# Loading the last unit of the output projection in three pieces: a half, a quarter and a quarter

## The chip, the cores and the metric

The kernel runs on one core of one Trainium2 chip. The metric is the device time in microseconds (us) of one execution. All runs quoted here are "fast" (within 1.5% of the fastest run of the same kernel). Beside the time, a run has a *span*, the time from the first to the last instruction of the profile; clock times such as "385.95" are microseconds from the start of that span.

Engines by the profile's names: PE is TensorE, DVE is VectorE, ACT is ScalarE, POOL is GpSimd, SP is SyncE, which here only issues loads. "16 engines" always means the 16 DMA engines that move the data. Each of them adds one to a load's semaphore (a counter) when it has finished its part; a load has *landed* when the sixteenth increment is there.

## The reference

One decode step of grouped attention, added to a small gated mixer. Cut to what matters:

```python
x = A_x                                            # [1, 1, 1024]
g = sigmoid((x * gate_w).sum(-1))
q = x @ wq                                         # 32 heads of 128
scores = einsum(q, k_cache) * 128 ** -0.5          # 4 kv heads, 65536 keys each
o = softmax(scores) @ v_cache                      # 32 x 128 = 4096 numbers
a = o @ wo                                         # wo: [4096, 1024]: "the output projection"
b = mixer(x, w_in, w_sp, b_sp, w_out)
return g * a + (1 - g) * b
```

There is one query, so every byte of the caches and weights (162 MB) is read once and used a few times: the kernel is a stream of loads with arithmetic behind it. `wo` (8 MB) comes last, because it is multiplied with the attention's result.

## The kernel before

All large loads go through one list, `stream`. The SP engine issues them in order into a ring of five slots (`NS = 5`); an issue waits until the former contents of its slot have been used. `wo` is four units of 2 MB, 16 KB of each of the 128 partitions.

```python
    for i in range(4):
        load([("wo", i)], [(0, rows(A_wo, i, 8))])
    # ... (cut)
    def issue(upto):
        while issued[0] < min(upto, len(stream)):
            n = issued[0]
            # ... (cut)
            P("SP", f, w=[("slot", s)], dma="s%d" % s)   # f: dma_start into slot n % NS
            issued[0] += 1
    # ... (cut)
    def done(key):                                       # called when a unit has been used
        n = place[key][0]
        if key == stream[n][0][-1]:
            issue(n + NS + 1)
```

The end of the program multiplies the four units with the attention's result `ovec` and adds the mixer's row `brow`:

```python
    FB = KTB[0]
    for i in range(4):
        sl, key = use(("wo", i))
        def f(e, i=i, sl=sl):
            for c in range(8):
                for q in range(4):
                    ins = e.matmul(pf(FB)[32 * q:32 * q + 1, 0:QW], ovec[:, 8 * i + c:8 * i + c + 1],
                                   sl[:, DO * c + QW * q:DO * c + QW * (q + 1)],
                                   start=(i == 0 and c == 0), stop=(i == 3 and c == 7), tile_position=(0, 32 * q),
                                   skip_group_check=True)
            return ins
        P("PE", f, r=[("ovec", i), key], w=[B(FB)])      # waits for the whole unit
    P("DVE", lambda e: e.tensor_tensor(orow[0:97, :], pf(FB)[0:97, 0:QW], brow[0:97, :], ALU.add),
      r=["brow"], w=["orow", B(FB)])
    # ... (cut) SP stores orow to the output
```

The four matmuls of one `c` use four different column groups of the array. In the trace they start within 15 ns of each other: below they are called a *round*. A unit is 8 rounds.

Of the kernel before, what the change touches and what calls it, by code (L numbers as in the profile page):

```python
# [137 lines left out]
def bass_gated_mix__gqa_block_cached__mixer_gmlp__decode_kernel(  # L138
# [19 lines left out]
    DO = A_wo.shape[1]  # L158
# [13 lines left out]
    QW = DO // 4  # L172
# [54 lines left out]
    def slot(n):  # L227
        return ab("RING", SLOT, (n % NS) * SLOT)
# [15 lines left out]
    def B(i):  # L244
        return ("bank", i)
# [12 lines left out]
    def small(dst, src, key):  # L258
        def f(e):
            with nc.allow_non_contiguous_dma(reason="a few bytes"):  # L260
                return e.dma_start(dst, src)
        P("ACT", f, w=[key], dma=key)
# [11 lines left out]
    def load(keys, pieces):  # L274

        for i, key in enumerate(keys):
            place[key] = (len(stream), i)
        stream.append((keys, pieces))

    def rows(w, i, c):  # L280

        return w[128 * c * i:128 * c * (i + 1), :].rearrange("(p c) n -> p (c n)", c=c)
# [28 lines left out]
    for n in range(NU, total + NU + 1):  # L311
# [7 lines left out]
        else:  # L319
            v = None  # L320
        steps.append((k, v, ()))
    for i in range(4):
        load([("wo", i)], [(0, rows(A_wo, i, 8))])

    WIDTH = {"wq": 2 * WQ_N, "win": 2 * F, "wout": 7 * DO, "wo": 8 * DO, "k": UK, "v": UK}
    issued = [0]
# [2 lines left out]
# [3 lines that stand above are left out]
            assert n < NS or all(k in used for k in stream[n - NS][0])  # L332
            keys, pieces = stream[n]
            s = n % NS

            def f(e, n=n, pieces=pieces):
                for c0, src in pieces:
                    ins = e.dma_start(slot(n)[:, c0:c0 + src.shape[1]], src)
                return ins
            P("SP", f, w=[("slot", s)], dma="s%d" % s)  # L340
            issued[0] += 1

    def use(key):
        n, i = place[key]
        issue(n + 1)
        used.add(key)
        w = WIDTH[key[0]]
        return slot(n)[:, i * w:(i + 1) * w], ("slot", n % NS)

    def done(key):  # L350
# [4 lines that stand above are left out]
# [25 lines left out]
    for i in range(4):  # L380
        sl, key = use(("wq", i))

        def f(e, i=i, sl=sl):
            for k in range(2):
                for h in range(HQ):
                    ins = e.matmul(pf(OB)[:, h:h + 1], sl[:, WQ_N * k + 128 * h:WQ_N * k + 128 * (h + 1)],  # L386
                                   xT[:, 2 * i + k:2 * i + k + 1], start=(i == 0 and k == 0 and h == 0),
                                   stop=(i == 3 and k == 1), skip_group_check=True)
            return ins
        P("PE", f, r=["xT", key], w=[B(OB)])  # L390
        done(("wq", i))
# [220 lines left out]


    FB = KTB[0]
    for i in range(4):
        sl, key = use(("wo", i))

        def f(e, i=i, sl=sl):
            for c in range(8):
                for q in range(4):  # L620
                    ins = e.matmul(pf(FB)[32 * q:32 * q + 1, 0:QW], ovec[:, 8 * i + c:8 * i + c + 1],  # L621
                                   sl[:, DO * c + QW * q:DO * c + QW * (q + 1)],
                                   start=(i == 0 and c == 0), stop=(i == 3 and c == 7), tile_position=(0, 32 * q),
                                   skip_group_check=True)
            return ins
        P("PE", f, r=[("ovec", i), key], w=[B(FB)])
    P("DVE", lambda e: e.tensor_tensor(orow[0:97, :], pf(FB)[0:97, 0:QW], brow[0:97, :], ALU.add),
      r=["brow"], w=["orow", B(FB)])
    osrc = bass.AP(tensor=arena, offset=OFF["OROW"], ap=[[32 * NA, 4], [1, QW]])
# [31 lines left out]
```

## Time and profile before

| | before |
|---|---|
| time, median of the first 3 runs | 392.74 us (392.17 to 393.21) |
| span of the profiled run | 390.4 us |
| load queue's share of the 16 engines' span | 97.1% |
| PE busy | 274.1 us, 70% |
| last load's last byte reported | 385.81 |
| last 32 matmuls | 385.95 to 387.83 |
| final add starts | 387.88 |

From the page of the kernel before: the DMA busy share in 40 slices of the span (tenths, 9 is 90% or more), the packet count, and two of the DMA queues (packets, MB, share of the 16 engines' span). Queue 1 carries the loads; queue 8 carries instructions.

```profile
DMA  8999999999999999999999999999999999999992
...
DMA packets 6778, 162.54 MB, mean 416 GB/s; under 512 B 1492, under 2 KB 1496, under 8 KB 1496
...
q1 hardware_dynamic: 5912, 162.01, 97.1%
q8 instruction: 30, 0.49, 0.5%
```

The kernel is bound by its loads. The digits are 9 from the second slice to the second last, and queue 1 alone takes 97.1%. What can be saved without moving fewer bytes is looked for here at the end of the stream. The end, from the chain of waits (start us, us, what):

```profile
361.59 24.22 DMA arena<-in_A_wo_dram
385.81 0.14 issue
385.95 1.91 PE pb L621 x32
...
387.88 0.42 DVE arena L627
```

The PE waits for unit 3 until 385.81, then does 1.91 us of matmuls, then the add follows. The timeline of the same stretch (start us, us, engine, line, operation, output<-input, count, and in brackets the idle time before it and what ended it):

```profile
374.50 3.58 PE L621 MATMUL pb<-arena 128*1 128x256 bf16 x64
...
380.99 1.04 PE L621 MATMUL pb<-arena 128*1 128x256 bf16 x32 [2.92 <-DMA arena<-in_A_wo_dram]
...
385.95 1.88 PE L621 MATMUL pb<-arena 128*1 128x256 bf16 x32 [3.91 <-DMA arena<-in_A_wo_dram]
387.88 0.42 DVE L627 TENSOR_TENSOR arena<-pb,arena 97x256 bf16<-97x256 f32 x1 [12.56 <-PE pb L621]
```

Units 0 and 1 run together at 374.50 because their data was there before the PE was free. Units 2 and 3 each wait for their load. Unit 3's group takes 1.88 us where unit 2's identical group took 1.04 us. The windows show the granted clock and the DMA share:

```profile
core 0: us, PE busy (x) PEld busy (x) DVE busy (x) ACT busy (x) POOL busy (x), PEclk, DMA share, GB/s
375.00:380.00 5.00, 3.08 (x60) 1.60 (x52) 0.32 (x1) 0.00 (x0) 0.00 (x0) 0.63 1.01 433
380.00:385.00 5.00, 1.04 (x32) 0.67 (x32) 0.00 (x0) 0.00 (x0) 0.00 (x0) 0.72 0.51 220
385.00:391.00 6.00, 1.88 (x32) 0.96 (x32) 0.42 (x1) 0.00 (x0) 0.00 (x0) 0.50 0.00 0
```

The last three columns are the granted TensorE clock, the DMA share and GB/s. The clock is a mean over the stretch. The trace's clock records have it at 1.0 from 378.74 to 382.16, while unit 2's group ran, and at 0.5 afterwards, while unit 3's ran: hence 1.04 and 1.88 us for the same work. From 375 to 380 all engines work (a share of about 1.0). From 380 to 385 only half the capacity is used, although unit 3 is still arriving. The reason is in the trace's records of semaphore increments. For unit 3 the first increment came at 380.48 and the sixteenth at 385.81. The engines run 5.3 us apart, and the load counts as there when the slowest is done.

### The profile page before, as it was taken

What the parts mean: (1) busy time and instruction counts of PE and PEld (TensorE: products, weight loads), DVE (VectorE), ACT (ScalarE), POOL (GpSimd) and SP (SyncE); (2) the same over time, 40 slices, a digit from 0 to 9 for tenths busy, and PEclk for the clock granted to TensorE, in tenths of its full rate; (3) what the DMA queues carried; (4) which work ended last, traced back from release to release, by engine and by line L of the source; (5) the groups of instructions that cost most, each with busy time, mean ns of one, the idle gap of its engine ahead of it and who ended that gap; (6) DMA issues with size and microseconds to landing.
All of it is one profiled execution on the core that took longest, in us unless ns stands there. A gap on an engine that the chain in (4) does not pass through costs nothing.

```text
span 390.4 us, 8502 instructions
## 1 busy us (share of the span) xinstructions
PE 274.1 (70%) x3902; PEld 194.6 (50%) x3902; DVE 160.2 (41%) x347; ACT 124.4 (32%) x171; POOL 1.5 (0%) x8
## 2 busy tenths in 40 slices
PE   0000699996999899976787596957974959574552
PEld 0000678885776676745565474645743736221121
DVE  2000043435666666644664263536742636410020
ACT  1000033332556555551355151613551425231000
POOL 1000000000000000000000000000000000000000
PEclk9999998685999999996899598968995989856555
DMA  8999999999999999999999999999999999999992
GB/s 322 430 430 437 418 412 441 426 428 425 411 405 431 433 426 431 428 431 428 427 431 428 428 431 430 425 435 435 428 431 433 428 426 431 433 431 421 416 415 96
DMA packets 6778, 162.54 MB, mean 416 GB/s; under 512 B 1492, under 2 KB 1496, under 8 KB 1496
## 3 DMA queue, kind: packets, MB, share of 16 engines
q1 hardware_dynamic: 5912, 162.01, 97.1%
q8 instruction: 30, 0.49, 0.5%
q10 hardware_dynamic: 832, 0.00, 0.1%
q14 instruction: 4, 0.03, 0.0%
HBM read 162.01 MB, written 0.00 MB: 415 GB/s over the span
## 4 chain that ended last, share of the span: by engine, by line
DMA 55%; PE 36%; DVE 6%; issue 1%; ACT 1%; ACTq 0%; DVEq 0%
DMA arena<-in_A_k_cache_dram 31%; PE pb L411 18%; DMA arena<-in_gate_w_dram 10%; DMA arena<-in_A_v_cache_dram 8%; PE pb L433 6%; DMA arena<-in_A_wo_dram 6%; PE pb L526 3%; DVE arena L419 3%; PE pb L478 3%; PE pb L386 2%; DVE arena L438 2%; PE pb L466 1%; ACT arena L416 0%; PE pb L621 0%; PE pb L574 0%
## 5 line engine op out<-in xcount | busy, mean ns | idle before, releaser
L411 PE MATMUL pb<-arena 128*128 128x128 bf16 x2048 | 153.6, 235 | 31.7 <-DMA arena<-in_A_k_cache_dram 31.7
L411 PEld LDWEIGHTS pb<-arena 128*128 128x128 bf16 x2048 | 131.9, 106 | 60.1 <-DMA arena<-in_A_k_cache_dram 34.7
L419 DVE COPY arena<-pb 128x1024 bf16<-128x1024 bf16 x160 | 108.3, 689 | 111.2 <-PE pb L411 110.2
L416 ACT ACTIVATE arena<-pb 128x1024 bf16<-128x1024 bf16 x96 | 98.0, 1021 | 162.2 <-PE pb L411 162.2
L433 PE MATMUL pb<-arena 128*32 128x512 bf16 x512 | 55.0, 420 | 6.1 <-DVE arena L438 4.2
L478 PE MATMUL pb<-arena 128*32 128x512 bf16 x512 | 39.9, 440 | 14.5 <-DMA arena<-in_A_v_cache_dram 10.5
L371 PE MATMUL pb<-arena 128*128 128x1 f32 x2 | 0.6, 362 | 41.0 <-DVE arena L370 41.0
L478 PEld LDWEIGHTS pb<-arena 128*32 128x32 bf16 x512 | 14.0, 104 | 28.5 <-issue 13.5
L459 ACT ACTIVATE arena<-arena 128x512 bf16<-128x512 f32 x32 | 22.8, 713 | 14.3 <-PE pb L466 12.6
L469 DVE COPY arena<-pb 128x512 bf16<-128x512 bf16 x32 | 13.6, 424 | 28.4 <-PE pb L466 28.4
L433 PEld LDWEIGHTS pb<-arena 128*32 128x32 bf16 x512 | 13.3, 93 | 22.9 <-DVE arena L438 7.7
L438 DVE TENSOR_SCALAR_CACHE_REDUCE arena<-pb 128x512 f32<-128x512 f32 x32 | 21.8, 682 | 2.8 <-PE pb L433 2.8
L371 PEld LDWEIGHTS pb<-arena 128*128 128x128 f32 x2 | 0.5, 313 | 41.0 <-DVE arena L370 41.0
L369 DVE TENSOR_TENSOR arena<-arena 128x8 f32<-128x8 bf16 x1 | 0.2, 168 | 37.2 <-DMA arena<-in_gate_w_dram 37.2
L466 PE MATMUL pb<-arena 128*128 128x128 bf16 x128 | 14.8, 248 | 0.0
L466 PEld LDWEIGHTS pb<-arena 128*128 128x128 bf16 x128 | 8.7, 109 | 11.4 <-issue 10.6
L526 PEld LDWEIGHTS pb<-arena 128*128 128x128 bf16 x224 | 13.6, 158 | 0.5 <-issue 0.5
L526 PE MATMUL pb<-arena 128*128 128x1 bf16 x224 | 13.8, 198 | 0.0
L373 ACT ACTIVATE arena<-pb 128x1 f32<-128x1 f32 x1 | 0.2, 171 | 37.0 <-PE pb L371 37.0
L621 PE MATMUL pb<-arena 128*1 128x256 bf16 x128 | 6.5, 379 | 6.8 <-DMA arena<-in_A_wo_dram 6.8
L386 PE MATMUL pb<-arena 128*128 128x1 bf16 x256 | 7.1, 165 | 2.1 <-issue 2.1
L621 PEld LDWEIGHTS pb<-arena 128*1 128x1 bf16 x128 | 3.6, 108 | 9.4 <-issue 4.4
(78 smaller groups left out, 59.7 us busy)
## 6 DMA issues: line engine op xcount, KB each, us to landing
arena<-in_A_k_cache_dram SPq DMA_DIRECT2D x16, 4096.0 KB, 30.2
arena<-in_A_v_cache_dram SPq DMA_DIRECT2D x16, 4096.0 KB, 31.7
arena<-in_A_wq_dram SPq DMA_DIRECT2D x2, 4096.0 KB, 17.4
arena<-in_A_wo_dram SPq DMA_DIRECT2D x4, 2048.0 KB, 30.1
arena<-in_B_w_in_dram SPq DMA_DIRECT2D x2, 3584.0 KB, 28.0
arena<-in_B_w_out_dram SPq DMA_DIRECT2D x1, 3584.0 KB, 17.3
arena<-in_A_x_dram ACTq DMA_DIRECT2D x1, 2.0 KB, 22.4
arena<-in_gate_w_dram ACTq DMA_DIRECT2D x1, 2.0 KB, 39.2
```

What stands on the lines that cost most here:

```text
L386: ins = e.matmul(pf(OB)[:, h:h + 1], sl[:, WQ_N * k + 128 * h:WQ_N * k + 128 * (h + 1)], xT[:, 2 * i + k:2 * i + k + 1], start=(i == 0 and ...
L411: ins = e.transpose(pbf(pb)[:, 128 * t:128 * (t + 1)], sl[:, 128 * (8 * b + t):128 * (8 * b + t + 1)], idb)
L416: P("ACT", lambda e, i=i, pb=pb: e.activation(ktb(i), pbf(pb), ACTF.Copy), w=[("kt", i % NKTS), B(pb)])
L419: P("DVE", lambda e, i=i, pb=pb: e.tensor_copy(ktb(i), pbf(pb)), w=[("kt", i % NKTS), B(pb)])
L433: ins = e.matmul(pf(SCB)[32 * cg:32 * (cg + 1), :], qpad[:, 128 * g + 32 * j:128 * g + 32 * (j + 1)], src, start=(j == 0), stop=(j == 3), ...
L438: P("DVE", lambda e: e.tensor_scalar(scs(n), pf(SCB), 0.0, None, op0=ALU.add, op1=ALU.max, accum_out=maxc[:, n:n + 1]), w=[("sc", n % NSC) ...
L459: P("ACT", lambda e: e.activation(psb(n), scs(n), ACTF.Exp, bias=gcol(g, K_NB), scale=SCALE, accum_out=lp[:, n:n + 1]), r=[("sc", n % NSC) ...
L466: ins = e.transpose(pbf(PTB)[:, 128 * xi:128 * (xi + 1)], psb(n)[:, 128 * xi:128 * (xi + 1)], idb)
L469: P("DVE", lambda e: e.tensor_copy(ptsb(n), pbf(PTB)[:, 0:512]), w=[("ptsb", n % 2), B(PTB)])
L478: ins = e.matmul(pf(OB)[32 * cg:32 * (cg + 1), :], ptsb(n)[:, 128 * xi + 32 * cg:128 * xi + 32 * (cg + 1)], vw(sl, 128 * (4 * cg + xi), [[ ...
L526: ins = e.matmul(pf(MB)[:, z:z + 1], vw(sl, c0, [[FC, 128]]), xT[:, 2 * i + k:2 * i + k + 1], start=(i == 0 and k == 0 and z == 0), stop=( ...
L621: ins = e.matmul(pf(FB)[32 * q:32 * q + 1, 0:QW], ovec[:, 8 * i + c:8 * i + c + 1], sl[:, DO * c + QW * q:DO * c + QW * (q + 1)], start=(i ...
```

## The change

The intent: when the last bytes land, less work should be left. Unit 3 is loaded as three pieces (8, 4 and 4 KB of each partition), each into a ring slot of its own with that slot's semaphore, and the matmuls of a piece wait for that piece alone. The arithmetic and its order stay.

```diff
-    for i in range(4):
-        load([("wo", i)], [(0, rows(A_wo, i, 8))])
+    WO = [(0, 0, 8), (1, 0, 8), (2, 0, 8), (3, 0, 4), (3, 4, 6), (3, 6, 8)]
+    for i, c0, c1 in WO:
+        load([("wo", i, c0)], [(0, rows(A_wo, i, 8)[:, DO * c0:DO * c1])])
 ...
-    for i in range(4):
-        sl, key = use(("wo", i))
-        def f(e, i=i, sl=sl):
-            for c in range(8):
+    for i, c0, c1 in WO:
+        sl, key = use(("wo", i, c0))
+        def f(e, i=i, sl=sl, c0=c0, c1=c1):
+            for c in range(c0, c1):
                 for q in range(4):
+                    o = DO * (c - c0) + QW * q
 ...             (the matmul reads sl[:, o:o + QW]; else as before)
         P("PE", f, r=[("ovec", i), key], w=[B(FB)])
+        done(("wo", i, c0))
```

There are now six loads and five slots. The sixth load takes the slot of unit 0, so SP issues it only after unit 0's matmuls; the added `done` lets it.

## The prediction

> What bounds the kernel. The DMA stream: queue 1 takes 97.1% of the 16 engines' span (queue table), and the 40 slices show DMA at 9 tenths to the second last. The chain of waits ends: 24.22 us for an A_wo load (361.59 to 385.81), 1.91 us of 32 matmuls on the last unit (from 385.95), 0.42 us of the vector add (387.88), then the output store; the span ends at 390.4. Only the 1.9 us of matmuls after the last landing can be hidden.
>
> The end in detail. The trace's semaphore increments show that the 16 engines run apart: the fastest finished the last 2 MB unit 5.3 us before the slowest (increments from 380.5 to 385.8). So the windows show a DMA share of about 1.0 until 380, then 0.6 falling to 0.3 until 385. The Trainium skill (DMA: Bandwidth & Descriptors, "Why a DMA increments its semaphore by 16 and not by 1") says that only the full 16 means all data landed; the trace agrees: the PE starts 0.14 us after the sixteenth increment.
> The PE idles 3.91 us before the last group (timeline). Its 32 matmuls run as 8 rounds of 4, one every 0.214 us, at a granted clock of 0.50.
>
> What the change does. Loads 0 to 2 stay. Load 3 becomes 8, 4 and 4 KB of each partition in place of 16, each with its own semaphore; the same PE work in the same order waits as 16 + 8 + 8 matmuls.
> - Removed: after the last landing 2 rounds remain in place of 8: 6 x 0.214 = 1.28 us (half at clock 1.0).
> - Added: each engine moves 24 data packets in place of 8. Packets took 613 ns for 16384 B and 1214 ns for 32768 B, so I estimate 12 ns fixed each: 16 x 12 = 0.19 us, plus two semaphore packets of 9 ns. The last landing moves to about 386.0.
> - Estimate for the slowest engine: half lands at 383.4, first quarter 384.7, last 386.0. The half needs about 1.1 us, a quarter 0.65 us: each is done before the next lands.
> - Moved: the ring has five slots, so the sixth piece waits for the matmuls of unit 0, done at about 376.3. [...] The fastest engine reaches it at about 379, the slowest at 384.5, so the engine that counts should not starve. The fifth's slot is free at 371.3, early enough.
>
> Critical path. Net 1.28 - 0.2 = about 1.05 us, all on the path: 0.27%. Predicted 391.7 us against 392.74, range 390.9 to 392.7. The runs of before spread over 1.04 us, as much as the gain.
>
> What the profile would show. DMA packets up by about 256 plus some tens for semaphores; the last group of output matmuls is 8, busy about 0.65 us instead of 1.88; the A_wo wait in the chain ends at 385.9 to 386.2; the vector add starts about 386.7. The sixth load is issued at about 376.4, the fifth near 371.4.
>
> What would make it wrong. The sixth load starts later than I think, or the slow engines reach it sooner: a gap in the DMA share near 378 to 380 and no gain, or a loss of about 1 us. Small packets cost more: at 50 ns each the gain shrinks to 0.4 us. A granted clock of 1.0 at the end of most runs of before would leave half the gain. The skill (TensorE: Matmul & The Clock Gate, "Part 1: The HAM clock gate") says that recent activity sets the clock; the trace agrees (1.00 after the burst of 374.5 to 378.1, 0.50 after the idle time).

## The result

| | before | after |
|---|---|---|
| time, median (same session) | 392.98 us (4 runs, 392.17 to 393.64) | 392.03 us (4 runs, 391.38 to 392.40) |
| ratio of the fast runs | | 0.9975 (95%: 0.9951 to 0.9999) |
| span of the profiled run | 390.4 us | 390.3 us |
| unit 2's matmuls start | 380.99 | 382.27 |
| final add starts | 387.88 | 387.82 |
| from unit 2's matmuls to the final add | 6.89 us | 5.55 us |

Ratios here and below are the mean time of one kernel's fast runs over that of the other's fast runs of the same rounds, so they are not quite the ratio of the medians quoted. The kernel is 0.25% faster, about 1.0 us, and the interval just excludes 1.

The page after: packets and queues.

```profile
DMA packets 7068, 162.56 MB, mean 416 GB/s; under 512 B 1525, under 2 KB 1529, under 8 KB 1785
...
q1 hardware_dynamic: 6200, 162.01, 97.2%
q8 instruction: 31, 0.51, 0.5%
...
q14 instruction: 5, 0.03, 0.0%
```

290 more packets: 16 more for each engine (256), 16 for each of the two further completions (32), and two for instructions. The chain of waits after:

```profile
375.82 1.83 PE pb L623 x32
...
377.67 9.45 DMA arena<-in_A_wo_dram
387.12 0.04 issue
387.17 0.63 PE pb L623 x8
...
387.82 0.42 DVE arena L629
```

The last group of matmuls is 0.63 us in the chain instead of 1.91. The timeline after:

```profile
375.75 3.58 PE L623 MATMUL pb<-arena 128*1 128x256 bf16 x64
...
382.27 1.88 PE L623 MATMUL pb<-arena 128*1 128x256 bf16 x32 [2.93 <-DMA arena<-in_A_wo_dram]
...
384.78 1.74 PE L623 MATMUL pb<-arena 128*1 128x256 bf16 x24 [0.64 <-DMA arena<-in_A_wo_dram]
...
387.17 0.60 PE L623 MATMUL pb<-arena 128*1 128x256 bf16 x8 [0.65 <-DMA arena<-in_A_wo_dram]
387.82 0.42 DVE L629 TENSOR_TENSOR arena<-pb,arena 97x256 bf16<-97x256 f32 x1 [11.25 <-PE pb L623]
```

The 24 matmuls at 384.78 are the half and the first quarter (their waits fall inside the merged line); the last quarter's 8 wait until 387.17 and take 0.60 us instead of 1.88. The windows after (columns as before):

```profile
375.00:380.00 5.00, 4.12 (x68) 2.25 (x68) 0.83 (x3) 0.00 (x0) 0.00 (x0) 0.50 0.98 401
380.00:385.00 5.00, 2.09 (x40) 1.10 (x44) 0.00 (x0) 0.00 (x0) 0.00 (x0) 0.50 0.51 211
```

At first sight the two profiles contradict each other: the work after the last landing shrank by 1.28 us, yet the add starts at nearly the same time (387.82 against 387.88) and the spans are equal. The row "unit 2's matmuls start" explains it. Unit 2 is loaded the same way in both kernels, and it landed 1.28 us later in the profiled run of the changed kernel. In that run the engines were 7.2 us apart when unit 2 landed, in that of before 5.4 us. The slowest engine was later well before anything of the change happened: at a load that landed near 318 to 319, the engines were 7.1 us apart in that run and 5.3 us in the other. So absolute clock times of two single profiles can't be compared to a microsecond. A better yardstick starts at the last point that both kernels share: **the time from unit 2's matmuls to the final add**. It is 6.89 us before and 5.55 us after, 1.34 us less.

### The profile page after: what moved, and what is told of

It is laid out like the page before. It is cut to its first block, busy times and chain, and to the rows that moved or that the text cites. A ratio compares the mean times of both kernels' runs of the same rounds, so it can differ in the third digit from the quotient of the medians.

```text
span 390.3 us, 8504 instructions
## 1 busy us (share of the span) xinstructions
PE 270.7 (69%) x3902; PEld 192.3 (49%) x3902; DVE 159.9 (41%) x347; ACT 124.3 (32%) x171; POOL 1.5 (0%) x8
## 4 chain that ended last, share of the span: by engine, by line
DMA 53%; PE 37%; DVE 7%; issue 1%; ACT 1%; ACTq 0%; DVEq 0%
DMA arena<-in_A_k_cache_dram 31%; PE pb L412 19%; DMA arena<-in_gate_w_dram 10%; DMA arena<-in_A_v_cache_dram 9%; PE pb L434 6%; DVE arena L420 4%; PE pb L527 3%; PE pb L479 3%; DMA arena<-in_A_wo_dram 2%; PE pb L387 2%; DVE arena L439 2%; PE pb L467 1%; PE pb L623 1%; ACT arena L417 0%; PE pb L575 0%
## 5 line engine op out<-in xcount | busy, mean ns | idle before, releaser
L412 PE MATMUL pb<-arena 128*128 128x128 bf16 x2048 | 151.8, 233 | 35.6 <-DMA arena<-in_A_k_cache_dram 35.6
L412 PEld LDWEIGHTS pb<-arena 128*128 128x128 bf16 x2048 | 130.6, 105 | 63.6 <-DMA arena<-in_A_k_cache_dram 39.1
L434 PE MATMUL pb<-arena 128*32 128x512 bf16 x512 | 54.3, 414 | 6.1 <-DVE arena L439 4.2
L479 PE MATMUL pb<-arena 128*32 128x512 bf16 x512 | 38.4, 426 | 16.4 <-DMA arena<-in_A_v_cache_dram 12.4
L467 PE MATMUL pb<-arena 128*128 128x128 bf16 x128 | 14.4, 243 | 0.0
L527 PEld LDWEIGHTS pb<-arena 128*128 128x128 bf16 x224 | 13.6, 159 | 0.5 <-issue 0.5
L467 PEld LDWEIGHTS pb<-arena 128*128 128x128 bf16 x128 | 8.4, 107 | 10.4 <-issue 10.0
L623 PE MATMUL pb<-arena 128*1 128x256 bf16 x128 | 7.7, 412 | 4.3 <-DMA arena<-in_A_wo_dram 4.2
L387 PEld LDWEIGHTS pb<-arena 128*128 128x128 bf16 x256 | 7.2, 105 | 2.5 <-issue 2.5
```

The lines of the kernel that those rows point to most:

```text
L387: ins = e.matmul(pf(OB)[:, h:h + 1], sl[:, WQ_N * k + 128 * h:WQ_N * k + 128 * (h + 1)], xT[:, 2 * i + k:2 * i + k + 1], start=(i == 0 and ...
L412: ins = e.transpose(pbf(pb)[:, 128 * t:128 * (t + 1)], sl[:, 128 * (8 * b + t):128 * (8 * b + t + 1)], idb)
L434: ins = e.matmul(pf(SCB)[32 * cg:32 * (cg + 1), :], qpad[:, 128 * g + 32 * j:128 * g + 32 * (j + 1)], src, start=(j == 0), stop=(j == 3), ...
L467: ins = e.transpose(pbf(PTB)[:, 128 * xi:128 * (xi + 1)], psb(n)[:, 128 * xi:128 * (xi + 1)], idb)
L479: ins = e.matmul(pf(OB)[32 * cg:32 * (cg + 1), :], ptsb(n)[:, 128 * xi + 32 * cg:128 * xi + 32 * (cg + 1)], vw(sl, 128 * (4 * cg + xi), [[ ...
L527: ins = e.matmul(pf(MB)[:, z:z + 1], vw(sl, c0, [[FC, 128]]), xT[:, 2 * i + k:2 * i + k + 1], start=(i == 0 and k == 0 and z == 0), stop=( ...
```

## The experiments

The theory (T1 in the expectations): at the end the cost is the *number of rounds after the last landing times the time of a round at the granted clock*; the split hides 6 of 8 rounds, and nothing else matters much. Rivals: the first result was luck, from the drift of the engines (R1); the smaller loads themselves land earlier (R2); the late sixth issue, or each further load, costs time that the split could have had (R3).

All outputs are right. Each kernel of this section is an edit of the kernel before or after. halves, finer, eighths and warm_before ran on one chip, the other experiments on a second one; the ratios are of one chip, but the yardsticks are compared across both. "2 to add" is the yardstick above; "2 to 3" is the time between the sixteenth increments of unit 2 and of the last piece of unit 3, from the trace; "clock there" is the granted clock while the last group ran; times are medians of 6 fast runs (4 for the row "after").

| kernel | rounds after the last landing | clock there | 2 to 3, us | 2 to add, us | time, us | ratio to before (95%) |
|---|---|---|---|---|---|---|
| before (profiled run) | 8 | 0.5 | 4.87 | 6.89 | | |
| after (profiled run) | 2 | 0.5 | 4.90 | 5.55 | 392.03 | 0.9975 (0.9951 to 0.9999) |
| after_again | 2 | 0.5 | 4.94 | 5.59 | 391.22 | 0.9953 (0.9934 to 0.9972) |
| one_wait | 8 | 0.5 | 4.90 | 6.92 | 393.33 | 1.001 (0.9989 to 1.003) |
| same_slot | 2 | 0.5 | 4.91 | 5.56 | 391.51 | 0.9965 (0.9946 to 0.9984) |
| late_issue | 2 | 0.5 | 6.06 | 6.70 | 392.14 | 0.9981 (0.9958 to 1.0003) |
| halves | 4 | 0.5 | 4.91 | 5.99 | 391.42 | 0.9962 (0.9944 to 0.998) |
| finer | 1 | 0.5 | 4.96 | 5.40 | 391.77 | 0.9961 (0.9945 to 0.9977) |
| eighths | 1 | 1.0 | 5.12 | 5.44 | 391.22 | 0.9946 (0.9931 to 0.9961) |
| warm_before | 8 | 1.0 | 4.85 | 6.04 | 392.32 | 0.997 (0.9952 to 0.9988) |
| warm_after | 2 | 1.0 | 4.91 | 5.36 | 391.71 | 0.9964 (0.9936 to 0.9991) |
| best | 1 | 1.0 | 4.99 | 5.32 | 391.41 | 0.9951 (0.9926 to 0.9977) |
| extra_instr | 2 | 0.5 | 4.96 | 5.61 | 400.31 | 1.018 (1.0152 to 1.0208) |

The timing has intervals of about 0.2% on each side, 0.7 us. It separates groups (one_wait from after_again) but not 0.2 us; such differences are read from the yardstick, which is one profile for each kernel.

### after_again: the changed kernel once more

No edit.

> The changed kernel itself, timed again. Theory T1 (the gain is the 6 rounds of matmuls that no longer follow the last landing, 1.28 us at clock 0.5, less the cost of more packets): 0.25 to 0.35% faster than before (about 1.0 to 1.3 us), and in the profile the time from the start of unit 2's matmuls to the start of the final add is about 5.5 us (5.55 in the first profile, 6.89 before). Rival R1 (the first measurement was luck: the 16 DMA engines drift apart by a different amount in every run): ratio within 0.1% of 1, and that time varies by as much as 1 us.

Measured: 391.22 us, ratio 0.9953; unit 2 to add 5.59 us. The timeline of this run:

```profile
381.20 1.09 PE L623 MATMUL pb<-arena 128*1 128x256 bf16 x32 [3.04 <-DMA arena<-in_A_wo_dram]
...
386.14 0.59 PE L623 MATMUL pb<-arena 128*1 128x256 bf16 x8 [0.65 <-DMA arena<-in_A_wo_dram]
386.79 0.42 DVE L629 TENSOR_TENSOR arena<-pb,arena 97x256 bf16<-97x256 f32 x1 [11.59 <-PE pb L623]
```

What follows: R1 falls. The yardstick repeats within 0.04 us, although the lag of the engines when unit 2 landed was 5.6 us here and 7.2 us there, and the ratio is below 1 again, with an interval clear of 1. The two measured gains, about 1.0 us and 1.85 us (0.47% of 393.1), lie on both sides of the 1.34 us of the yardstick, and both intervals hold it.

### one_wait: three loads, one wait

```diff
+        keys = [key] if i < 3 or c0 else [use(("wo",) + w[:2])[1] for w in WO if w[0] == 3]
-        P("PE", f, r=[("ovec", i), key], w=[B(FB)])
+        P("PE", f, r=[("ovec", i)] + keys, w=[B(FB)])
```

> The same three loads, but the 32 matmuls of unit 3 start only when all three pieces have landed. T1: no gain is left: same as before, or 0.0 to 0.2 us slower (16 more packets for each engine), and 6.9 to 7.1 us from unit 2's matmuls to the add. Rival R2 (the gain comes from the loads themselves: smaller transfers land earlier): still about 1 us faster than before, about 5.5 to 6 us.

Measured: 393.33 us, ratio 1.001; unit 2 to add 6.92 us.

```profile
383.16 1.88 PE L623 MATMUL pb<-arena 128*1 128x256 bf16 x32 [3.07 <-DMA arena<-in_A_wo_dram]
...
388.15 1.88 PE L623 MATMUL pb<-arena 128*1 128x256 bf16 x32 [3.12 <-DMA arena<-in_A_wo_dram]
390.08 0.42 DVE L630 TENSOR_TENSOR arena<-pb,arena 97x256 bf16<-97x256 f32 x1 [12.83 <-PE pb L623]
```

What follows: R2 falls. With the loads in pieces but a common wait, 32 matmuls (1.88 us) follow the last landing as before, and the gain is gone. The pieces alone cost 0.03 us at the end (4.90 against 4.87 us from unit 2 to unit 3).

### same_slot: no late issue

Unit 3's pieces go into different parts of one slot, with a semaphore for each piece.

```diff
-        load([("wo", i, c0)], [(0, rows(A_wo, i, 8)[:, DO * c0:DO * c1])])
+        if i < 3:
+            load([("wo", i, c0)], [(0, rows(A_wo, i, 8)[:, DO * c0:DO * c1])])
+    last = [w for w in WO if w[0] == 3]
+    load([("wo", 3, a) for _, a, b in last], [(DO * a, rows(A_wo, 3, 8)[:, DO * a:DO * b]) for _, a, b in last])
 ...             (SP issues these three one after the other, each with its own semaphore)
```

> The three pieces go into the slot of unit 3 with a semaphore each, so all three are issued when that slot is free and none waits for unit 0's matmuls. T1, with the late sixth issue hidden by the lag of the slowest engine: the same as the changed kernel within 0.15% (5.5 us from unit 2 to the add), while the fastest engine no longer has a gap (its last piece comes 1.25 us after the one before it, not 1.55). Rival R3 (the late issue costs time): 0.2 to 0.4 us faster than the changed kernel.

Measured: 391.51 us, ratio 0.9965; unit 2 to add 5.56 us. The first increment of the last piece came 1.25 us after the first of the piece before (379.64 to 380.89); in the profile of the changed kernel it came 1.55 us after (378.80 to 380.35), in after_again 1.25 us. In that profile of the changed kernel, taken in order, the first six increments came 1.55 to 2.11 us after those of the piece before, and the seventh 1.24 us after.

What follows: the late sixth issue costs nothing that shows at the end. In one of two profiles it made six engines wait, 0.3 to 0.9 us, and that ended before the slowest engine was done.

### late_issue: the sixth load held back further

```diff
-            P("SP", f, w=[("slot", s)], dma="s%d" % s)
+            P("SP", f, r=["tok"] if n == len(stream) - 1 else [], w=[("slot", s)], dma="s%d" % s)
 ...
-        P("PE", f, r=[("ovec", i), key], w=[B(FB)])
-        done(("wo", i, c0))
+        P("PE", f, r=[("ovec", i), key], w=[B(FB)] + (["tok"] if i == 2 else []))
+        if i == 2:
+            done(("wo", i, c0))
```

The token `tok` is written by unit 2's matmuls and read by the sixth issue; `done` is called after unit 2 alone, so that no earlier one triggers it.

> The sixth load is held back on purpose until unit 2's matmuls are done, about 6.5 us later than in the changed kernel. If only the slowest engine counts, then what matters is whether it still has work by then: it reaches its last piece about 3.2 us after unit 2 landed, unit 2's matmuls take 1.0 (clock 1.0) to 1.9 us (clock 0.5), and the load needs about 1.0 us from issue to its first packet: at most 0.3 us slower than the changed kernel, although the fast engines idle some 5 us each. Rival R3 (any gap in the stream costs its length): 3 to 6 us slower than the changed kernel.

Measured: 392.14 us, ratio 0.9981 against 0.9953 of the changed kernel: 0.28%, 1.1 us slower. The two intervals overlap, but the yardstick says the same, 6.70 against 5.59 us.

```profile
380.93 1.88 PE L623 MATMUL pb<-arena 128*1 128x256 bf16 x32 [3.32 <-DMA arena<-in_A_wo_dram]
382.85 0.33 SPq L339 DMA_DIRECT2D arena<-in_A_wo_dram  x1
...
383.49 1.75 PE L623 MATMUL pb<-arena 128*1 128x256 bf16 x24 [0.69 <-DMA arena<-in_A_wo_dram]
...
386.98 0.59 PE L623 MATMUL pb<-arena 128*1 128x256 bf16 x8 [1.74 <-DMA arena<-in_A_wo_dram]
387.63 0.42 DVE L630 TENSOR_TENSOR arena<-pb,arena 97x256 bf16<-97x256 f32 x1 [13.17 <-PE pb L623]
```

The sixth load was issued at 382.85 instead of about 376.3, 6.5 us later; 1.1 us of that came through to the end. So the rival of 3 to 6 us is wrong: most of the delay is absorbed by the lag of the slowest engine. But my bound of 0.3 us is wrong too. The trace shows why: the first packet ran at 383.85, 1.0 us after the issue, as expected, and the slowest engine had work until about 384.2. But into an empty queue the load did not run at its usual pace: some of its 4 KB packets, normally 159 ns, took up to 1.03 us, and the increments came between 385.56 and 386.94. From issue to the last increment it took 4.1 us; the same piece behind a full queue came 1.25 us after its predecessor. By this run the issue would have had to come at least 1.1 us earlier, some 2.5 us before the slowest engine gets to the piece (an estimate: 384.2 less 382.85, plus the 1.1 us lost). The change keeps far more: its sixth issue came at 377.67 and the slowest engine finished the piece before it at 385.88.

### halves, finer, eighths: other cuts

```diff
-    WO = [(0, 0, 8), (1, 0, 8), (2, 0, 8), (3, 0, 4), (3, 4, 6), (3, 6, 8)]
+    WO = [(0, 0, 8), (1, 0, 8), (2, 0, 8), (3, 0, 4), (3, 4, 8)]                        # halves
+    WO = [(0, 0, 8), (1, 0, 8), (2, 0, 8), (3, 0, 4), (3, 4, 6), (3, 6, 7), (3, 7, 8)]  # finer
+    WO = [(0, 0, 8), (1, 0, 8), (2, 0, 8), (3, 0, 1), (3, 1, 2), ... (3, 7, 8)]         # eighths, as same_slot
```

> Unit 3 in two halves of 8 KB of each partition. T1 (after the last landing only the rounds of the last piece remain, 0.214 us each at clock 0.5): 4 of 8 rounds are hidden, 0.85 us, less 0.03 us for packets: about 6.05 us from unit 2's matmuls to the final add (6.89 before, 5.55 with a half and two quarters), about 0.2% faster than before. Rival R2 (the number or size of the loads matters, not the work after the last): no such proportion, for example the full 5.55.

Measured: 391.42 us, ratio 0.9962; unit 2 to add 5.99 us (6.05 expected).

```profile
380.83 1.04 PE L623 MATMUL pb<-arena 128*1 128x256 bf16 x32 [2.93 <-DMA arena<-in_A_wo_dram]
...
385.75 1.02 PE L623 MATMUL pb<-arena 128*1 128x256 bf16 x16 [1.34 <-DMA arena<-in_A_wo_dram]
386.82 0.42 DVE L629 TENSOR_TENSOR arena<-pb,arena 97x256 bf16<-97x256 f32 x1 [11.68 <-PE pb L623]
```

> Unit 3 in a half, a quarter and two eighths; the sixth and seventh loads wait for the slots of units 0 and 1. T1: one round remains after the last landing, 7 x 0.214 = 1.50 us hidden less about 0.1 for packets and semaphores: about 5.4 us from unit 2 to the add, 0.2 us less than the changed kernel; too little for the timing to tell from it (about 0.35% faster than before). Rival R3 (each further load costs a fixed 0.2 us or more at the end): 5.6 us or more.

Measured: 391.77 us, ratio 0.9961; unit 2 to add 5.40 us (5.4 expected).

> Unit 3 in eight loads of 2 KB of each partition, all in its own slot and issued together. T1: one round remains (1.50 us hidden), but each engine has 64 packets for 8; if each costs 6 ns more than its share, as the 4 KB packets did (159 ns against a quarter of 613), 0.3 us goes back: about 5.7 us from unit 2 to the add, no better than the changed kernel. If packets of 2 KB cost much more (50 ns), over 8 us and slower than before.

Measured: 391.22 us, ratio 0.9946; unit 2 to add 5.44 us (5.7 expected). From unit 2 to unit 3 took 5.12 us, 0.25 us more than before, near the 0.3 expected. So packets explain 0.05 us of the surprise. The clock explains 0.10: the trace has the granted clock at 1.0 from 384.31 to 387.72 in this run, and the last group took 0.31 us in the chain where finer's took 0.41 at 0.5. Another 0.10 is the wait between landing and first matmul, which is explained under "The sum" below.

What follows: the yardstick goes with the rounds that remain. From 8 to 4 it fell by 0.90 us, from 4 to 2 by 0.40 to 0.44, from 2 to 1 by 0.15 to 0.19. Each further cut is worth half of the one before, and from the eighths on the packets take back what the last round gives. The timing of these kernels can't be told from that of the changed one.

### warm_before, warm_after: the round's other factor

Useless matmuls into a bank of the accumulator memory (PSUM) that is no longer needed, ahead of each wait, are meant to raise the clock. In warm_before they are in the kernel before, without any split.

```diff
+    WARM = {2: 6, 3: 10}                                            # warm_before
+    WARM = {(2, 0): 6, (3, 0): 3, (3, 4): 1, (3, 6): 1}             # warm_after
 ...
+        def warm(e, m=WARM.get(i, 0)):
+            for _ in range(m):
+                ins = e.matmul(pf(SCB), idb, sel, start=True, stop=True)
+            return ins
+        if i in WARM:
+            P("PE", warm, r=["idb", "sel"], w=[B(SCB)])
```

> The kernel before, with 6 useless 128x512 matmuls ahead of unit 2's and 10 ahead of unit 3's, in time that the PE spent waiting, so that the granted clock is 1.0 at the end. T1 says that the cost is rounds after the last landing times the time of a round at the granted clock: 8 rounds of about 0.107 in place of 0.214 us, so 0.8 to 0.85 us less (about 6.05 us from unit 2's matmuls to the add), 0.2% faster, with no load split at all. Rival (the clock records do not matter here, or the clock does not rise): 6.9 us, no gain, or a loss if the added matmuls run into the landing.

Measured: 392.32 us, ratio 0.997; unit 2 to add 6.04 us. The timeline, with the 10 useless matmuls in the second line:

```profile
382.64 1.04 PE L629 MATMUL pb<-arena 128*1 128x256 bf16 x32 [1.00 <-DMA arena<-in_A_wo_dram]
...
383.62 2.33 PE L621 MATMUL pb<-arena 128*128 128x512 bf16 x10
...
387.58 1.04 PE L629 MATMUL pb<-arena 128*1 128x256 bf16 x32 [1.63 <-DMA arena<-in_A_wo_dram]
388.68 0.42 DVE L635 TENSOR_TENSOR arena<-pb,arena 97x256 bf16<-97x256 f32 x1 [11.73 <-PE pb L629]
```

> The changed kernel with useless 128x512 matmuls in the PE's idle time (6 ahead of unit 2, 3 ahead of the half, 1 ahead of each quarter), so that the granted clock is 1.0 at the end. T1: only 2 rounds are left after the last landing, so a clock of 1.0 saves 2 x 0.107 us and a little latency: about 5.3 us from unit 2's matmuls to the add (5.55 to 5.59 without), against the 0.85 us that the same clock gave the kernel before. Rival (the two remedies add up): about 4.7 us, 0.5% faster than before.

Measured: 391.71 us, ratio 0.9964; unit 2 to add 5.36 us.

```profile
381.68 1.04 PE L631 MATMUL pb<-arena 128*1 128x256 bf16 x32 [1.31 <-DMA arena<-in_A_wo_dram]
...
386.59 0.39 PE L631 MATMUL pb<-arena 128*1 128x256 bf16 x8 [0.53 <-DMA arena<-in_A_wo_dram]
387.04 0.42 DVE L637 TENSOR_TENSOR arena<-pb,arena 97x256 bf16<-97x256 f32 x1 [11.07 <-PE pb L631]
```

What follows: the clock is a second factor of the same product. In warm_before the granted clock was 1.0 from 380.74 to 390.98, the last 32 matmuls took 1.04 us instead of 1.88, and the end became 0.85 us shorter without a single load split. On top of the split the same clock saved 0.19 to 0.23 us. The remedies do not add up, because both shorten the same stretch. With the clock at 1.0 the split is worth 6.04 - 5.36 = 0.68 us, half of its 1.34.

### best: the remedies together

```diff
+    WO as in finer, loads as in same_slot, WARM = {(2, 0): 6, (3, 0): 3, (3, 4): 1, (3, 6): 1}
```

> A half, a quarter and two eighths in the slot of unit 3, all issued together, with the same useless matmuls. One round at clock 1.0 remains after the last landing: about 5.3 us from unit 2 to the add, 0.2 to 0.3 us less than the changed kernel; 0.3 to 0.45% faster than before. The timing can't tell it from the changed kernel.

Measured: 391.41 us, ratio 0.9951; unit 2 to add 5.32 us. By the yardstick it is the shortest end of all, 0.23 to 0.27 us shorter than the changed kernel's; by the timing it is faster than before and not distinguishable from the changed kernel.

### extra_instr: where the lag of the engines comes from

The lag of 5 to 7 us is larger than anything that the change saves, and it differs from run to run. In the trace it grows in steps. The instruction queue has 30 packets of 16 KB before, on the same 16 engines, and about 1 us after nearly every one of them there is one 32 KB load packet that took about 1.7 us in place of 1.21. The experiment adds instructions that do nothing, on the idle POOL engine:

```diff
+    def idle(e):
+        for _ in range(6144):                     # builds to 3072 instructions of two waits each
+            e.wait_ge(R.dsem["xT"], 16)           # long fulfilled
+    P("POOL", idle, r=["xT"])
```

> The changed kernel with 3072 further instructions on the idle POOL engine (semaphore waits that are long fulfilled). Theory of the lag (each 16 KB instruction fetch runs on one of the 16 DMA engines and holds up that engine's share of the stream by 0.6 to 1.1 us, and the engine with the most fetches ends last): about 12 more fetches, the slowest engine ends 0.5 to 3 us later, the spread of the engines at the end grows from 5 to 7 us to 6 to 9 us, and the kernel is 0.1 to 0.8% slower than the changed one. Rival (the lag comes from the memory or from the data transfers themselves): the same as the changed kernel within 0.1%.

Measured: 400.31 us, ratio 1.018, against 0.995 to 0.996 of two kernels that carry the split: 2.2%, some 9 us. Queues of its page (packets, MB, share):

```profile
q1 hardware_dynamic: 6200, 162.01, 95.4%
q8 instruction: 31, 0.51, 0.5%
q14 instruction: 28, 0.23, 0.1%
```

Queue 14 has 28 instruction packets of 8 KB by the trace, in place of 4 (the fifth on the page after has 96 bytes). The 24 new ones come about every 11.6 us. One takes 0.31 us, and the 32 KB load packet that starts as it ends takes 1.57 us in place of 1.21. The last two increments of the same load show who paid:

```
increments of one load, us after its first (landing near 356 to 366)
after_again:  ... 5.1 5.2 5.2  5.3
extra_instr:  ... 5.8 5.9 6.1 15.5
```

Fifteen engines are about where they were, and one is over 9 us behind them. Its lag grew steadily from 2.0 us at 60 us to 15.5 us at about 300 us, while the waits ran, and stayed there afterwards. The end of the kernel waits for this engine. The sizes fit: 24 fetches of 0.31 + 0.36 us are 16 us.

What follows: the lag comes from instruction fetches, at least what was added here. The direction was expected, the size was not: I had expected 12 fetches of 16 KB, spread over the engines; there were 24 of 8 KB, and all of the added ones held up the same engine. The rival (memory, or the transfers themselves) predicted no change. That the waits themselves, and not their fetches, held up this engine was not tested by a run; that its lag grew fetch by fetch, by the size of a fetch, speaks against it. For the other kernels, a 16 KB fetch took about 1.06 us and the packet after it 0.49 us more; by these numbers three or four fetches on one engine would make a lag of 5 us (an estimate). That all of their lag has this cause is likely, but it was not tested by taking instructions away.

## Why the prediction was right

Point by point:

- **Total.** Predicted 391.7 us, range 390.9 to 392.7. Measured 392.03, and 391.22 in a second session; both in the range. That the first came so close is in part luck: its gain of about 1.0 us has an interval from 0.0 to 1.9 us, and the upper end of the predicted range lies just under the 392.74 us of before. What bears out the prediction is the yardstick and one_wait.
- **What is removed: 6 rounds, 1.28 us.** Right. The last group went from 1.88 to 0.60 us, exactly 1.28. one_wait shows it as the cause: the same loads without this part gain nothing. halves (4 rounds hidden) and finer (7 hidden) lie on the same line.
- **What is added: 0.2 us for packets.** The mechanism was right and the size was off. The 16 further packets of an engine were put at 12 ns each, from a line through the times of 16 KB and 32 KB packets, which did not hold below them. Measured: 309 ns for 8 KB and 159 ns for 4 KB, that is 2.5 and 6 ns over their share of 613; and the last landing moved by 0.03 us in the first profile (4.90 against 4.87) and by 0.08 in the second.
- **The sum.** 1.28 - 0.03 gives 1.25; the yardstick fell by 1.34. The difference is in the chain's "issue" line between landing and first matmul: 0.14 us before, 0.04 us after. The traces' records of waits show what differs. The first group that uses unit 3 waits for two things, its load and VectorE's `ovec`: a wait instruction of its own for the load (385.84 in the kernel before), then the first weight load with the other wait (385.92). A later piece has one wait, on its weight load. The line is 0.14 us in the three kernels whose last group has the pair (before, one_wait, warm_before) and 0.04 in all the others. The prediction did not have this 0.10 us; it and the smaller cost of packets make the gain larger than the 1.05 us predicted.
- **The pipeline of the pieces.** Right: each piece was done before the next landed. In the timeline after, the PE sat idle for 0.65 us before the last quarter.
- **The moved issue.** Issued at 377.67 in the first profile and at 376.31 in the second (376.4 predicted). Right that the engine that counts would not starve. That the fast ones would wait (0.3 to 0.9 us in one profile) was named only among what could make it wrong, with a loss of the gain; they waited, and the gain stayed. late_issue shows the limit: 6.5 us later it costs 1.1 us.
- **Clock times of the end.** "The A_wo wait ends at 385.9 to 386.2" and "the add starts about 386.7" did not hold in the first profile (387.12 and 387.82) and did in the second (386.10 and 386.79). The step that failed was to take the lag of the slowest engine, 5.3 us in one trace, as a property of the kernel. It was 7.2 us in the next one.
- **The clock's half.** "Half at clock 1.0" was right: 0.68 us between the two warm kernels, 1.34 between the two cold ones. The Trainium skill (TensorE: Matmul & The Clock Gate, "Part 1: The HAM clock gate") gives 3413 ns as the window over which activity is watched. The clock records agree: the complete periods of one clock are multiples of 3.41 us (10.24 us in warm_before, 23.89 us in the kernel before).

## What to carry to other kernels

When a stream of loads bounds a kernel, the work after the last landing is on the critical path: cut the last load so that little of it remains, and give each piece a wait of its own, because the pieces without the waits gain nothing. In this kernel its cost was the rounds left times the time of a round at the granted clock, so a clock of 1.0 and a small last piece compete for the same microsecond, and after a half and two quarters little is left (at most 0.27 us by the yardstick). Before reading a microsecond off two profiles, line them up at the last event that both kernels share, since the landing of the same load can differ by more than the change is worth.

## What the Trainium skill lacked or had wrong

- Runtime: NRT & Kernel Launch, "Instruction fetch mechanics": it calls the cost of crossing a block of instructions "mostly hidden". It may be so for the sequencer, but not for a saturated load stream: 24 more fetches put one DMA engine over 9 us behind the others and made the kernel 2.2% slower. The page gives blocks of 16 KiB; POOL's packets here were of 8 KB, those of queue 8 of 16 KB.
- DMA: Bandwidth & Descriptors, "Why a DMA increments its semaphore by 16 and not by 1": it says that the engines finish independently, but not how far apart. Here 4.9 to 7.2 us at the end of a 390 us stream without the added instructions, and 15.5 us with them, against 0.7 us for the first loads of the kernel before.
- The same page, "Bandwidth", advises loads of at least 1 MiB, from measurements with GpSimd issuing. For pieces that SP issues behind a full queue that does not bind: 1 MB, 0.5 MB and 0.5 MB cost 0.03 to 0.08 us more than one load of 2 MB, eight of 0.25 MB cost 0.25 us.
